# Agent attention with a squared-ReLU layer on one core: VectorE and ScalarE take over the element-wise work that GpSimd shared

## The chip, the core and the metric

The kernel runs on one core of a Trainium2 chip. The metric is the device time of one execution in microseconds (us). One execution was profiled; the times below name it apart from the other runs. Engine names: TensorE (PE in the rows, its weight loads PEld), VectorE (DVE), ScalarE (ACT), GpSimd (POOL), SyncE (SP, it issues the DMAs).

## The reference, cut to what matters

Four batches of 12480 tokens with 128 features, 49 agent tokens per batch, and a feed-forward layer of width 2048 behind the attention:

```python
a2k = sm(agents, k)                 # agents attend to the keys
agent_v = a2k @ v
q2a = sm(q, agents)                 # queries attend to the agents
x = (q2a @ agent_v).reshape(49920, 128)
h = np.maximum(x @ w_in, 0.0)
out = (h * h) @ w_out
```

All of it is float32. `sm` is a softmax of the scaled dot products.

## The kernel before, in words

The product `agent_v @ w_in` is made once per batch (the table `aw_hi`, with its low part `aw_ex`), so that a token's hidden values come straight from its 49 attention weights. Tokens go in blocks of 960, and each block in two halves of 480 columns; 52 blocks, 104 halves. The hidden width of 2048 is cut into 16 pieces of 128, two pieces make a slot, so a half has 8 slots and the kernel 832. Slots are grouped into sessions of 3, 3 and 2 (`SIZES`), three sessions per half.

One session of m slots does this:

- `first` (L351): 2m matmuls of the weights with `aw_hi` and 2m small ones with `aw_ex` (19 rows) into m PSUM tiles `h` of two banks. There are three such tiles, all of PSUM but the banks of `o` and `psa`.
- `squares` (L378): the rectifier of each slot into the tile `r`, then one square over the whole session on ScalarE. In a session of three, VectorE rectifies the first slot and ScalarE the other two.
- `halved` (L390): the squares are split in two parts that TensorE can take at full speed. `g_hi` is a rounding copy (VectorE). `g_lo` is the difference `r - g_hi`: the first m pieces of 480 columns on GpSimd (L394), one instruction each, and the other m pieces in one instruction on VectorE.
- `second` (L411): per piece of 128, two matmuls with `g_hi` (tables `wo_lo`, `wo_hi`) and, after all of those, one with `g_lo`, 6m in all, accumulated over the half in the one PSUM tile `o`. After the last session of a half `copied_out` (L401) copies `o` to `ob` on VectorE and sends it out; the next half's first `second` needs `o` back.

The order is written out by hand. `queued` chains each such instruction to the one before it on its engine. In step s of the main loop TensorE gets `first(s)` and then `second(s-2)` (`LAG = 2`); ScalarE gets rectifiers and squares of s; VectorE gets, in this order, the copy to `ob` if one is due and `halved(s-1)`.

Beside this runs the attention, as Python generators that are moved a step at a time: `queries` (scores of the block after next with the agents, softmax, splitting, transposes by TensorE, the copy `w`, then five DMAs per half that lay `w` out for the small matmuls) and `background` (scores, maxima, weighted values and tables of the next batch). They share the one PSUM bank `psa`. In the steady part `alone` is False, and then an instruction issued through `pe`, `act`, `dve`, `pool`, `sync` is not chained: the scheduler places it in its engine's queue where it expects its inputs to be ready. `tiled` matmuls are always chained. In `first`, a due step of `queries` or `background` is moved after the hidden matmuls, if the last transposes are more than a slot back or the session has three slots (`turns`).

```python
        for n in range(m):
            nc.gpsimd.tensor_sub(rest[:, n, :], r[:, n, :], near[:, n, :])
        n = slice(m, 2 * m)
        queued(nc.vector.tensor_sub, nc.vector, rest[:, n, :], r[:, n, :], near[:, n, :])
```

Of the kernel before, what the change touches and what calls it, by code (L numbers as in the profile page):

```python
# [18 lines left out]
TP = 120  # L19
# [2 lines left out]
KB = P * NT  # L22
G = BLK // 2
SIZES = (3, 3, 2)
WIDEST = max(SIZES)
RB = 3
HB = 2
# [14 lines left out]
def agent_attention_relu2(ctx: ExitStack, tc: tile.TileContext, qT, kT, v, agT, w_in, w_out, outT):  # L42
# [24 lines left out]
    alone = [True]  # L67

    class Ordered:
        def __init__(self, eng):  # L70
            self.eng = eng

        def __getattr__(self, name):
            issue = getattr(self.eng, name)
            if not alone[0]:
                return issue
            return lambda *args, **kw: queued(issue, self.eng, *args, **kw)

    pe, act, dve, pool, sync = (Ordered(e) for e in (nc.tensor, nc.scalar, nc.vector, nc.gpsimd, nc.sync))

    const = ctx.enter_context(tc.tile_pool(name="const", bufs=1))
    kv = ctx.enter_context(tc.tile_pool(name="kv", bufs=2))
# [100 lines left out]
    def scores(b, i, kt):  # L183
        st = state.setdefault(b, {"s": []})
        _, rows, nt = blocks[i]
        yield 3
        sv = bank()[:rows, : nt * NA].rearrange("p (t a) -> p t a", a=NA)
        for t in range(nt):
            tiled(sv[:, t, :], kt[:, t * rows : (t + 1) * rows], ag[:, b, :])
        s = sp.tile([P, 512], F32, name="s")[:, : NT * NA].rearrange("p (t a) -> p t a", a=NA)  # L190
        st["s"].append(s)
        if i == 0:
            st["mx"] = small.tile([P, NT, NA], F32, name="mx")
        s, mx = (x[:rows, :nt, :] for x in (s, st["mx"]))
        act.copy(s, sv)
        if i == 0:
            dve.tensor_copy(mx, s)
        else:
            dve.tensor_max(mx, mx, s)
# [48 lines left out]
    def values(b, i, vt):  # L248
        st = state[b]
        _, rows, nt = blocks[i]  # L250
        es = st["mx"][:rows, :nt, :]
        e = small.tile([P, NT, NA], F32, name="d", bufs=2)[:rows, :nt, :] if i else es
        less_maximum(b, i, e, pool)
        yield
        act.activation(e, e, AF.Exp, scale=scale)
        yield 3 if i else FIRST
        pv = bank()
        for t in range(nt):
            tiled(pv[:C, :NA], vt[:rows, t, :], e[:, t, :], start=(t == 0), stop=(t == nt - 1))
        if i == 0:  # L260
            st["av"] = small.tile([C, NA], F32, name="av")
            dve.tensor_copy(st["av"], pv[:C, :NA])
        else:
            dve.tensor_add(st["av"], st["av"], pv[:C, :NA])
            pool.tensor_add(es, es, e)  # L265

    def tables(b):
        st = state[b]
        rl, av = st["rl"], st["avT"]
        hi = st["hi"] = aw.tile([P, FF], F32R, name="aw_hi")  # L270
        ex = st["lo"] = aw.tile([P, NCH // NQ, P], F32R, name="aw_ex")
        for n in range(FF // 512):
            yield
            cs = slice(n * 512, (n + 1) * 512)
            pw = bank()
            pe.matmul(pw[:K2, :], av, win[:, cs], start=True, stop=True)
            yield
            act.activation(hi[:K2, cs], pw[:K2, :], AF.Copy, scale=rl)
            lo = aw.tile([P, 512], F32R, name="aw_lo", bufs=3)[:NA, :]
            dve.scalar_tensor_tensor(  # L280
                out=lo, in0=pw[:NA, :], scalar=rl[:NA, :], in1=hi[:NA, cs].bitcast(F32),
                op0=ALU.mult, op1=ALU.subtract,
            )
            yield
            sync.dma_start(hi[K2:, cs].bitcast(F32), lo[:SP, :].bitcast(F32))
            for t in range(NQ):
                sync.dma_start(ex[t * 32 : t * 32 + NL, n, :].bitcast(F32), lo[SP:, t * P : (t + 1) * P].bitcast(F32))


    weights = {}  # L290
    slot, turns = [0], [-2]

    def queries(g):
        b = g // NB
        qt = qp.tile([C, BLK], F32, name="qt", bufs=1)
        sync.dma_start(qt, qT[:, g * BLK : (g + 1) * BLK])
        yield 3
        ps = ps_a.tile([P, 512], F32, name="psa")
        sv = ps[:TP, : NT * NA].rearrange("p (t a) -> p t a", a=NA)
        for t in range(NT):  # L300
            tiled(sv[:, t, :], qt[:, t * TP : (t + 1) * TP], ag[:, b, :])
        if alone[0]:
            yield
        m = qp.tile([TP, NT, 1], F32, name="m", bufs=1)
        dve.reduce_max(m, sv, axis=AX.X)
        e = qp.tile([TP, NT, NA], F32, name="e", bufs=1)
        dve.tensor_sub(e, sv, m.broadcast_to([TP, NT, NA]))  # L307
        yield
        if not alone[0]:
            yield  # L310
        act.activation(e, e, AF.Exp, scale=scale)  # L311
        yield
        z = qp.tile([TP, NT, 1], F32, name="z", bufs=1)
        dve.reduce_sum(z, e, axis=AX.X)
        dve.tensor_scalar_add(z, z, 1e-9)
        dve.reciprocal(z, z)
        pool.tensor_mul(e, e, z.broadcast_to([TP, NT, NA]))  # L317
        yield
        pp = qp.tile([TP, NT, K2], F32R, name="pp", bufs=1)
        yield from halves(pp, e, NA, pool)  # L320
        weights[g] = []
        for j in range(2):
            yield
            pt = ps_a.tile([P, 512], F32, name="psa")
            turns[0] = slot[0]
            for t in range(NT // 2):
                pe.matmul(  # L327
                    pt[:K2, t * TP : (t + 1) * TP], pp[:, j * (NT // 2) + t, :], identr, start=True, stop=True
                )
            w = qp.tile([P, G], F32R, name=f"w{j}", bufs=2)  # L330
            x = qp.tile([P, G], F32R, name=f"x{j}", bufs=2)
            act.copy(w[:K2, :], pt[:K2, :G])  # L332
            weights[g].append((w, x))
            yield
            sync.dma_start(w[K2:, :].bitcast(F32), w[:SP, :].bitcast(F32))
            for t in range(NQ):
                sync.dma_start(x[t * 32 : t * 32 + NL, :].bitcast(F32), w[SP:NA, :].bitcast(F32))
# [9 lines left out]
    def first(k, m):  # L347
# [11 lines left out]
        with tc.high_priority():  # L359
            for n, out in outs:  # L360
                t = n % NQ
                rows = slice(t * 32, t * 32 + NL)
                queued(nc.tensor.matmul, nc.tensor, out, state[b]["lo"][rows, n // NQ, :], x[rows, :], start=False, stop=True)
        if turns[0] < k - 1 or m == WIDEST:
            for name in ("ahead", "todo"):
                if type(stands.get(name)) is int and k >= stands[name] and done[name] < goal[name]:
                    move(name, k)
                    break
        return hs

    def squares(hs, apart):

        m = len(hs)
        r = ffn.tile([P, WIDEST, 2, G], F32, name="r", bufs=RB)
        for x, h in enumerate(hs):
            if x == 0 and m == WIDEST:
                queued(nc.vector.tensor_scalar_max, nc.vector, r[:, x, :, :], h[:, :, :G], 0.0)
            else:  # L378
                queued(nc.scalar.activation, nc.scalar, r[:, x, :, :], h[:, :, :G], AF.Relu)
        for x in pieces(m, apart):  # L380
            queued(nc.scalar.activation, nc.scalar, r[:, x, :, :], r[:, x, :, :], AF.Square)
        return r

    def pieces(m, apart):
        return [slice(x, x + 1) for x in range(m)] if apart else [slice(0, m)]

    def halved(k, m, r, apart):
        hi = ffn.tile([P, WIDEST, 2, G], F32R, name="g_hi", bufs=HB)
        lo = ffn.tile([P, WIDEST, 2, G], F32R, name="g_lo", bufs=LB)
        for x in pieces(m, apart):  # L390
            queued(nc.vector.tensor_copy, nc.vector, hi[:, x, :, :], r[:, x, :, :])
        r, near, rest = (x.rearrange("p s n t -> p (s n) t") for x in (r, hi.bitcast(F32), lo))
        for n in range(m):
            nc.gpsimd.tensor_sub(rest[:, n, :], r[:, n, :], near[:, n, :])  # L394
        n = slice(m, 2 * m)
        queued(nc.vector.tensor_sub, nc.vector, rest[:, n, :], r[:, n, :], near[:, n, :])
        for x in range(m):
            parts[k + x] = hi[:, x, :, :], lo[:, x, :, :]

# [317 lines left out]
    following = [None]  # L717
    sessions, at = [], 0
    while at < total:
        for m in SIZES:  # L720
            sessions.append((at, m))
            at += m
    made, split = {}, {}
    for s in range(len(sessions) + LAG):
# [2 lines left out]
            behind = [chain[eng] for eng in (nc.tensor, nc.sync, nc.scalar, nc.vector, nc.gpsimd)]  # L727
        if m:
            between(k)
            hs = first(k, m)  # L730
        copied_out()
        if m:
            made[s] = squares(hs, s < LAG)
            if s < LAG:
                alone[0] = True
                if s:
# [4 lines left out]
            halved(*sessions[s - 1], made.pop(s - 1), s <= LAG)  # L741
        if s >= LAG:
            second(*sessions[s - LAG])
        for x in range(1, m):
            between(k + x)
    copied_out()
# [35 lines left out]
```

## Time and profile before

| what | value |
|---|---|
| median of 3 runs | 2259.98 us (2257.22 to 2265.25) |
| the profiled execution | 2256.87 us |
| its span | 2255.0 us |
| mean granted TensorE clock | 0.955 of full speed |
| busy: TensorE, VectorE, ScalarE, GpSimd | 89%, 72%, 64%, 76% |

The span runs from the first to the last instruction on the core; 1.87 us of the execution lie around it. Busy shares say how long an engine had an instruction in it, not how well the instruction ran: matmuls are pipelined and overlap, so their spacing tells more than their duration. In a timeline row, the square brackets give the idle time of the engine before the instruction and what ended it; "x6" merges six instructions of one kind.

### The profile page before, as it was taken

The numbers are of one execution on the slowest core, as the hardware profiler recorded it, in microseconds if no ns is written. First come the engines' busy times: TensorE is split into PE (matmuls) and PEld (weight loads), VectorE is DVE, ScalarE is ACT, GpSimd is POOL, SyncE is SP. The second block draws the span as 40 slices with busy tenths as digits, with TensorE's granted clock in tenths as the row PEclk, the third lists the DMA queues.
The fourth block names the chain that finished last, engine by engine and source line by source line (L and its number), as shares of the span: only waits on it lengthen the run. The fifth ranks groups of instructions, "written<-read, shape, count | busy, mean of one in ns | idle before, by whom it ended". The sixth has DMA issues, their size and how long they took to land.

```text
span 2255.0 us, 41091 instructions
## 1 busy us (share of the span) xinstructions
PE 2004.8 (89%) x17181; PEld 1534.7 (68%) x17181; DVE 1626.9 (72%) x1400; ACT 1453.7 (64%) x1309; POOL 1716.7 (76%) x1033
## 2 busy tenths in 40 slices
PE   8888888899998898899989899889998989998898
PEld 5577666666676676676767676667666767666676
DVE  7677767677767677667768677667777777776776
ACT  5566666666765666666766666566676666766664
POOL 3567778877877778887777777888777887887787
PEclk9899999999999999999999999889999999999999
DMA  9122212111112222121112121121111110111100
GB/s 337 57 74 68 65 57 76 55 58 45 35 56 68 59 63 76 54 66 60 33 35 67 57 74 48 54 73 57 34 41 39 33 41 28 38 38 36 39 22 20
DMA packets 54829, 131.55 MB, mean 58 GB/s; under 512 B 6508, under 2 KB 34828, under 8 KB 54644
## 3 DMA queue, kind: packets, MB, share of 16 engines
q1 hardware_dynamic: 54644, 128.93, 17.8%
q8 instruction: 135, 2.21, 0.4%
q14 instruction: 50, 0.41, 0.1%
HBM read 80.97 MB, written 25.56 MB: 47 GB/s over the span
## 4 chain that ended last, share of the span: by engine, by line
PE 38%; POOL 34%; DVE 10%; issue 9%; ACT 9%; DMA 0%; ACTq 0%; SPq 0%; POOLq 0%; DVEq 0%
POOL g_lo L394 29%; PE o L63 23%; PE h L63 12%; ACT r L63 7%; DVE g_hi L63 5%; POOL e L317 3%; DVE r L63 3%; PE psa L63 2%; ACT w L332 1%; POOL d L231 1%; DMA ahead<-in_kT 0%; DVE t L63 0%; DVE mx L63 0%; POOL mx L265 0%; POOL pp L225 0%
## 5 line engine op out<-in xcount | busy, mean ns | idle before, releaser
L394 POOL TENSOR_TENSOR g_lo<-r,g_hi 128x480 fp32r<-128x480 f32 x832 | 1475.8, 1802 | 458.1 <-DVE g_hi L63 393.2
L63 ACT ACTIVATE r<-h 128x960 f32<-128x960 f32 x624 | 571.3, 969 | 306.2 <-PE h L63 291.8
L63 ACT ACTIVATE r<-r 128x2880 f32<-128x2880 f32 (+2 forms) x316 | 733.6, 2323 | 11.1 <-DVE r L63 3.1
L63 PE MATMUL o<-g_hi,wo_lo 128*128 128x480 f32 x1664 | 693.1, 416 | 49.2 <-DVE ob L63 49.2
L63 PE MATMUL o<-g_hi,wo_hi 128*128 128x480 f32 x1664 | 656.6, 395 | 0.0
L63 DVE TENSOR_TENSOR g_lo<-r,g_hi 128x1440 fp32r<-128x1440 f32 (+1 forms) x312 | 594.4, 1905 | 6.7
L63 DVE TENSOR_SCALAR r<-h 128x960 f32<-128x960 f32 x208 | 240.7, 1157 | 466.1 <-PE h L63 432.0
L63 DVE CAST g_hi<-r 128x2880 fp32r<-128x2880 f32 (+2 forms) x316 | 513.5, 1626 | 20.0 <-ACT r L63 17.9
L63 PE MATMUL o<-g_lo,wo_hi 128*128 128x480 f32 x1664 | 433.9, 388 | 44.8 <-POOL g_lo L394 44.4
L63 PE MATMUL h<-w,aw_hi 128*128 128x480 f32 x1664 | 442.1, 392 | 28.0 <-ACT r L63 20.3
L63 PEld LDWEIGHTS o<-g_hi,wo_lo 128*128 128x128 f32 x1664 | 329.2, 198 | 158.0 <-DVE ob L63 63.1
L63 PEld LDWEIGHTS o<-g_lo,wo_hi 128*128 128x128 f32 x1664 | 318.3, 193 | 111.7 <-POOL g_lo L394 63.3
L63 PEld LDWEIGHTS h<-w,aw_hi 128*128 128x128 f32 x1664 | 311.5, 192 | 89.4 <-ACT r L63 29.4
L63 PEld LDWEIGHTS o<-g_hi,wo_hi 128*128 128x128 f32 x1664 | 330.4, 199 | 44.1 <-issue 0.7
L63 PE MATMUL h<-x,aw_ex 19*128 19x480 f32 x1664 | 199.4, 458 | 0.0
L223 ACT CAST pp<-e 120x392 fp32r<-120x392 f32 x51 | 26.8, 525 | 249.1 <-POOL e L317 249.1
L63 PEld LDWEIGHTS h<-x,aw_ex 19*128 19x128 f32 x1664 | 82.4, 184 | 106.2 <-issue 104.0
L63 DVE COPY ob<-o 128x480 f32<-128x480 f32 x104 | 67.4, 648 | 45.7 <-PE o L63 45.7
L327 PEld LDWEIGHTS psa<-identr,pp 120*98 120x98 f32 x408 | 50.2, 176 | 62.3 <-ACT w L332 36.7
L327 PE MATMUL psa<-identr,pp 120*98 120x120 f32 x408 | 55.6, 262 | 39.9 <-ACT w L332 26.7
L225 POOL TENSOR_TENSOR pp<-e,pp 120x392 fp32r<-120x392 f32 x51 | 62.4, 1223 | 24.8 <-ACT pp L223 24.8
L311 ACT ACTIVATE e<-e 120x392 f32<-120x392 f32 x51 | 27.1, 531 | 82.5 <-DVE e L307 82.5
(143 smaller groups left out, 940.9 us busy)
## 6 DMA issues: line engine op xcount, KB each, us to landing
qt<-in_qT SPq DMA_DIRECT2D x52, 480.0 KB
out_T<-ob SPq DMA_DIRECT2D x104, 240.0 KB
kt<-in_kT SPq DMA_DIRECT2D x36, 512.0 KB
vt<-in_v SPq DMA_DIRECT2D x36, 512.0 KB
x<-w SPq DMA_DIRECT2D x416, 35.6 KB
ahead<-in_kT SPq DMA_DIRECT2D x12, 512.0 KB
ahead<-in_v SPq DMA_DIRECT2D x12, 512.0 KB
w<-w SPq DMA_DIRECT2D x104, 56.2 KB
```

The lines of the kernel that those rows point to most:

```text
L63: ins = issue(*args, **kw)
L223: act.copy(out[:, :, :w], x)
L225: eng.tensor_sub(out[:, :, n : n + w], x, out[:, :, :w].bitcast(F32))
L231: eng.tensor_sub(out, st["s"][i][:rows, :nt, :], mb)
L311: act.activation(e, e, AF.Exp, scale=scale)
L317: pool.tensor_mul(e, e, z.broadcast_to([TP, NT, NA]))
L327: pe.matmul(pt[:K2, t * TP : (t + 1) * TP], pp[:, j * (NT // 2) + t, :], identr, start=True, stop=True)
L332: act.copy(w[:K2, :], pt[:K2, :G])
L394: nc.gpsimd.tensor_sub(rest[:, n, :], r[:, n, :], near[:, n, :])
```

## The change

Seven edits. GpSimd keeps its work only while `alone` is True, that is, before the steady part; afterwards `spare()` is VectorE, and so four small subtractions, products and sums of the attention go there. `halved` makes the whole low part in one VectorE instruction per session. All rectifiers go to ScalarE, and they are issued inside `first`, ahead of the attention step that may follow there. The transposes of `queries` are chained, and their step waits (`"turn"`) until a `second` has been issued, directly behind which it is moved. Three ScalarE copies out of `psa` are chained (`fixed`). The condition with `turns` goes. The first half of all is cut into four sessions of two slots (`EARLY`).

```diff
+EARLY = (2, 2, 2, 2)
...
+    fixed = Ordered(nc.scalar, True)
+
+    def spare():
+        return pool if alone[0] else dve
...
-        act.copy(s, sv)
+        fixed.copy(s, sv)
...
-        less_maximum(b, i, e, pool)
+        less_maximum(b, i, e, spare())
...
-            pool.tensor_add(es, es, e)
+            spare().tensor_add(es, es, e)
...
-            act.activation(hi[:K2, cs], pw[:K2, :], AF.Copy, scale=rl)
+            fixed.activation(hi[:K2, cs], pw[:K2, :], AF.Copy, scale=rl)
...
-        pool.tensor_mul(e, e, z.broadcast_to([TP, NT, NA]))
+        spare().tensor_mul(e, e, z.broadcast_to([TP, NT, NA]))
         yield
         pp = qp.tile([TP, NT, K2], F32R, name="pp", bufs=1)
-        yield from halves(pp, e, NA, pool)
+        yield from halves(pp, e, NA, spare())
         weights[g] = []
         for j in range(2):
-            yield
+            yield "turn"
             pt = ps_a.tile([P, 512], F32, name="psa")
-            turns[0] = slot[0]
             for t in range(NT // 2):
-                pe.matmul(
-                    pt[:K2, t * TP : (t + 1) * TP], pp[:, j * (NT // 2) + t, :], identr, start=True, stop=True
+                queued(
+                    nc.tensor.matmul, nc.tensor, pt[:K2, t * TP : (t + 1) * TP], pp[:, j * (NT // 2) + t, :], identr, start=True, stop=True
                 )
...
-            act.copy(w[:K2, :], pt[:K2, :G])
+            fixed.copy(w[:K2, :], pt[:K2, :G])
...
-        if turns[0] < k - 1 or m == WIDEST:
-            for name in ("ahead", "todo"):
-                if type(stands.get(name)) is int and k >= stands[name] and done[name] < goal[name]:
-                    move(name, k)
-                    break
-        return hs
-
-    def squares(hs, apart):
-
-        m = len(hs)
         r = ffn.tile([P, WIDEST, 2, G], F32, name="r", bufs=RB)
         for x, h in enumerate(hs):
-            if x == 0 and m == WIDEST:
-                queued(nc.vector.tensor_scalar_max, nc.vector, r[:, x, :, :], h[:, :, :G], 0.0)
-            else:
-                queued(nc.scalar.activation, nc.scalar, r[:, x, :, :], h[:, :, :G], AF.Relu)
+            queued(nc.scalar.activation, nc.scalar, r[:, x, :, :], h[:, :, :G], AF.Relu)
+        for name in ("ahead", "todo"):
+            if type(stands.get(name)) is int and k >= stands[name] and done[name] < goal[name]:
+                move(name, k)
+                break
+        return r
+
+    def squares(m, r, apart):
         for x in pieces(m, apart):
             queued(nc.scalar.activation, nc.scalar, r[:, x, :, :], r[:, x, :, :], AF.Square)
-        return r
...
-        r, near, rest = (x.rearrange("p s n t -> p (s n) t") for x in (r, hi.bitcast(F32), lo))
-        for n in range(m):
-            nc.gpsimd.tensor_sub(rest[:, n, :], r[:, n, :], near[:, n, :])
-        n = slice(m, 2 * m)
-        queued(nc.vector.tensor_sub, nc.vector, rest[:, n, :], r[:, n, :], near[:, n, :])
+        for x in pieces(m, apart):
+            queued(nc.vector.tensor_sub, nc.vector, lo[:, x, :, :], r[:, x, :, :], hi[:, x, :, :].bitcast(F32))
...
-        for m in SIZES:
+        for m in SIZES if at else EARLY:
...
         if s >= LAG:
             second(*sessions[s - LAG])
+            if stands.get("ahead") == "turn":
+                move("ahead", slot[0])
```

## Rows read from the trace of the kernel before

**Rows 1.** The page: busy time, share of the span and instructions of each engine.
```profile
PE 2004.8 (89%) x17181; PEld 1534.7 (68%) x17181; DVE 1626.9 (72%) x1400; ACT 1453.7 (64%) x1309; POOL 1716.7 (76%) x1033
```

**Rows 2.** The page: the chain that ended last, by engine and by line.
```profile
PE 38%; POOL 34%; DVE 10%; issue 9%; ACT 9%; DMA 0%; ACTq 0%; SPq 0%; POOLq 0%; DVEq 0%
```

**Rows 3.** Tile ob: count, duration min/median/max in ns, first and last start; whole span, last quarter.
```profile
L63 DVE COPY ob<-o x104: 639/647/659, 101.7 to 2251.5; 128x480 f32<-128x480 f32 x104
...
L63 DVE COPY ob<-o x24: 641/650/658, 1800.3 to 2251.5; 128x480 f32<-128x480 f32 x24
```

**Rows 4.** Waits, all engines: who waited for whom, us in total, times, longest us.
```profile
POOL g_lo L394 <- DVE g_hi L63: 393.2, 144, 15.6
...
ACT pp L223 <- POOL e L317: 249.1, 51, 8.0
...
PE o L63 <- DVE ob L63: 49.2, 44, 1.7
...
PE o L63 <- POOL g_lo L394: 44.4, 30, 2.1
```

**Rows 5.** Timeline of TensorE, 1833 to 1856 us: start, duration, engine, line, operation.
```profile
1836.62 0.48 PE L327 MATMUL psa<-identr,pp 120*98 120x120 f32 x4
1836.94 1.09 PE L63 MATMUL h<-w,aw_hi 128*128 128x480 f32 x4
...
1843.52 1.12 PE L63 MATMUL o<-g_lo,wo_hi 128*128 128x480 f32 x4 [0.95 <-POOL g_lo L394]
1844.48 1.47 PE L63 MATMUL h<-w,aw_hi 128*128 128x480 f32 x6
...
1850.55 1.46 PE L63 MATMUL h<-w,aw_hi 128*128 128x480 f32 x6
...
1852.57 0.90 PE L63 MATMUL psa<-ag,qt 128*32 128x49 f32 x64
```

**Rows 6.** Timeline of TensorE, 605 to 632 us.
```profile
620.60 1.50 PE L63 MATMUL o<-g_lo,wo_hi 128*128 128x480 f32 x4 [2.08 <-POOL g_lo L394]
621.90 2.60 PE L63 MATMUL h<-w,aw_hi 128*128 128x480 f32 x6
```

**Rows 7.** Groups by form, the attention's matmuls: count, busy us, mean ns, idle before.
```profile
L63 PE MATMUL psa<-ag,qt 128*32 128x49 f32 x2496 | 47.2, 210 | 0.0
...
L63 PE MATMUL psa<-ag,kt 128*32 128x49 f32 x2340 | 36.5, 218 | 38.2 <-ACT w L332 21.6 <-issue 14.3 <-DVE e L307 2.3
L63 PE MATMUL psa<-d,vt 128*32 128x49 f32 x2112 | 35.7, 228 | 23.9 <-ACT w L332 13.1 <-issue 10.7
```

**Rows 8.** Groups by form, the element-wise work of the sessions.
```profile
L394 POOL TENSOR_TENSOR g_lo<-r,g_hi 128x480 fp32r<-128x480 f32 x832 | 1475.8, 1802 | 458.1 <-DVE g_hi L63 393.2 <-ACT r L63 21.3 <-DVE av L264 10.4
...
L63 ACT ACTIVATE r<-h 128x960 f32<-128x960 f32 x624 | 571.3, 969 | 306.2 <-PE h L63 291.8 <-POOL g_lo L394 14.4
L63 ACT ACTIVATE r<-r 128x2880 f32<-128x2880 f32 x206 | 539.3, 2618 | 8.3 <-DVE r L63 3.1
...
L63 DVE TENSOR_SCALAR r<-h 128x960 f32<-128x960 f32 x208 | 240.7, 1157 | 466.1 <-PE h L63 432.0 <-POOL g_lo L394 30.8 <-POOL mx L231 3.2
```

**Rows 9.** Timeline of VectorE, 1828 to 1862 us.
```profile
1835.28 1.66 DVE L63 CAST g_hi<-r 128x2880 fp32r<-128x2880 f32 x1 [0.24 <-ACT r L63]
1836.98 1.66 DVE L63 TENSOR_TENSOR g_lo<-r,g_hi 128x1440 fp32r<-128x1440 f32 x1
...
1840.17 2.23 DVE L63 CAST g_hi<-r 128x2880 fp32r<-128x2880 f32 x1 [0.96 <-ACT r L63]
1842.44 2.54 DVE L63 TENSOR_TENSOR g_lo<-r,g_hi 128x1440 fp32r<-128x1440 f32 x1
...
1849.47 1.16 DVE L63 TENSOR_TENSOR g_lo<-r,g_hi 128x960 fp32r<-128x960 f32 x1
...
1855.17 0.56 DVE L305 TENSOR_REDUCE m<-psa 120x8 f32<-120x392 f32 x1
...
1858.11 0.55 DVE L307 TENSOR_TENSOR e<-psa,m 120x392 f32<-120x392 f32 x1
```

**Rows 10.** Tile z: count, duration min/median/max in ns.
```profile
L315 DVE TENSOR_SCALAR z<-z x51: 165/1184/1196, 92.4 to 2182.7; 120x8 f32<-120x8 f32 x51
```

More of the change, by code (lines that the diff above doesn't have):

```diff
@@ L69, in agent_attention_relu2, with __init__ @@
     class Ordered:
-        def __init__(self, eng):
-            self.eng = eng
+        def __init__(self, eng, always=False):
+            self.eng, self.always = eng, always
         def __getattr__(self, name):
             issue = getattr(self.eng, name)
-            if not alone[0]:
+            if not (alone[0] or self.always):
                 return issue
@@ L290, in agent_attention_relu2 @@
     weights = {}
-    slot, turns = [0], [-2]
+    slot = [0]
     def queries(g):
@@ L729, in agent_attention_relu2 @@
             between(k)
-            hs = first(k, m)
+            made[s] = first(k, m)
         copied_out()
         if m:
-            made[s] = squares(hs, s < LAG)
+            squares(m, made[s], s < LAG)
             if s < LAG:
```

## The prediction, made before the changed kernel was run

> **What bounds the kernel now.** I read the busy shares first. TensorE stands at 89% and GpSimd at 76%, and no engine is full [rows 1]. The chain that ended last is split between TensorE (38%) and GpSimd (34%) [rows 2], so the end is set by an exchange between the two. The copies to `ob` then give the beat: 104 of them, the first at 101.7 us and the last at 2251.5, so 103 halves at 2149.8 / 103 = 20.87 us; in the last quarter, with no further batch to prepare, 23 halves in 451.2 us, 19.62 each [rows 3]. The waits say who holds whom: GpSimd waits 393 us for `g_hi`, ScalarE's rounding copy `pp` waits 249 us in its queue for GpSimd's product `e`, and TensorE waits for `g_lo` and for `ob` [rows 4].
>
> What would TensorE need if nothing held it? The 89% cannot tell. In the timeline a session of three slots takes from one `h` group to the next 1850.55 - 1844.48 = 6.07 us with no wait inside [rows 5]. A session of two has two thirds of the instructions, 4.05. A half is 2 x 6.07 + 4.05 = 16.2 us. The attention adds groups of 64 small matmuls at 0.90 us [rows 5]: 52 for queries (2496 / 48), 37 for keys (2340 / 64), 33 for values (2112 / 64) [rows 7], 110 us; and 102 groups of transposes at 1836.94 - 1836.62 = 0.32, 33 us. That is 1.4 per half. So TensorE needs **17.6 us** of the 20.87, and 3.3 per half are waits and slow clock. The Trainium skill warns of this very reading (Trainium Kernel Development and Optimization, Performance Expectations: matmul busy time is a bad measure of closeness, because matmuls are pipelined). Taken as work, 2004.8 us of busy time would allow no less than 19.3 us per half, and the sum below would end near 2100.
>
> The slow clock hangs on the waits: behind a wait of 2.08 us six `h` matmuls took 2.60 us, behind one of 0.95 they took 1.47 [rows 5, 6], the first at the 1.2 GHz level, the second at 2.4.
>
> **The change part by part.**
>
> *GpSimd's low parts.* 832 instructions of 1802 ns go [rows 8]; the second of two sessions of three waits for six in a row. What replaces them is one VectorE instruction per session, 2880 elements wide in a session of three, which no row shows. The nearest are 1.16 us for 960 and 1.66 for 1440 [rows 9], so 0.5 per 480, which gives 1.66 + 1.5 = **3.16 us**. The same form also took 2.54 [rows 9], when GpSimd was inside an instruction at its start; doubled that is 5.0, the upper end. Below 3.1 there is no reason to go. I take 3.16, since GpSimd will be idle; that the delay is GpSimd's, the 8-element instruction on `z` says, which takes 165 ns at best and 1184 in the median [rows 10].
>
> *Rectifiers.* VectorE loses 208 x 1157 ns, ScalarE gains 208 x about 0.92 (571.3 / 624, back to back) [rows 8]. VectorE is spared 2.3 us per half that stood ahead of a rounding copy; a session's three rectifiers now run one behind the other, 2.75 us where ScalarE's two took 1.83. They hide beside TensorE's `second` of 18 matmuls, about 3.9 us; if ScalarE comes late, `h` comes free late and the next `first` waits.
>
> *Four attention steps to VectorE.* 51 products, 51 differences, 36 differences and 33 sums, 171 at 0.55 (as `e` [rows 9]), 0.9 us per half. VectorE then has per half 2 x (1.66 + 3.16), two thirds of 4.82 for the small session, 0.65 for `ob`, 0.9, and some 1.5 of attention that it had: 15.9 us. ScalarE has (1453.7 + 191) / 104 = 15.8. Both lie under 17.6, so neither bounds by its sum; both are covers that get thin.
>
> *Transposes and `turn`.* Four matmuls, the copy `w` and then five DMAs on SyncE's queue move behind a `second`. Counting the steps, one per slot, the two turns fall in the second half of a block, at its first and second session, and the last DMAs are issued four slots before the weights are read, half a period or some 9 us. I cost them at nothing for the time; without that cover the first matmul of a block would wait. The chained ScalarE copies wait behind the squares ahead of them, and the next user of `psa` waits with them; it comes a `first` later, at least 1.3 us. Of the 249 us that `pp` waited for GpSimd [rows 4] I count nothing twice: they end in the waits already counted.
>
> *First half in two-slot sessions.* One more hand-over, smaller pieces, once; between -3 and +5 us, taken as 0: the first `ob` stays at 101.7.
>
> **What is late next.** The copy to `ob`. Once per half the accumulator must be copied before the next half's `second`. VectorE has the copy behind the whole `halved` of a three-slot session. From the moment that session's `h` is done: 2.75 rectifiers, 2.62 square [rows 8], 1.66 rounding copy, 3.16 low part, 0.65 `ob`, and some 0.25 for hand-overs: 11.1 us. TensorE meanwhile does a `second` and a `first` of three and of two: 6.07 + 4.05 = 10.1. It waits 1.0. In every other half the scores of a query lie in this stretch (TensorE +0.9), but `m` and `e` also come onto VectorE ahead of the copy (0.56 + 0.55 [rows 9]): wait 1.2. In the others two transposes lie in it (0.64): wait 0.4. On average 0.8 us, short enough that by the pair above the clock stays up.
>
> **The sum.** 17.6 + 0.8 = 18.4 us per half. 101.7 + 103 x 18.4 + 3.5 (behind the last `ob`) = 2000 us of span; with 1.9 around it 2002. The profiled execution lies 3.1 under the median of the runs, so the forecast for the median is **2005 us**, 11% less.
>
> **The rivals.**
>
> (1) *The background falls on the chain* (25%). The chain of 11.1 us runs through ScalarE and VectorE, and unchained attention steps are put into both queues by expectation. For it: `pp` stood waiting on ScalarE for 4.9 us on average (249.1 / 51 [rows 4]), and both engines now run at 86% of the new period. If half of the 1.5 us of ScalarE's and 2.4 of VectorE's attention work per half lands in it, that adds 1.9, of which TensorE's own background hides some: 1.2. Then 19.6 per half, 2005 + 103 x 1.2 = 2129. Against it: much of VectorE's time behind `ob` is free. The Trainium skill leans to this side (ScalarE: Activation LUTs, Rules for kernel authors: for relu use VectorE, not ScalarE). This trace has it the other way for this shape, 969 ns on ScalarE against 1157 on VectorE [rows 8]; only the load of ScalarE speaks for the rule.
>
> (2) *Everything is hidden* (14%). TensorE's background covers the wait for `ob` wholly: 17.6 per half, 1923.
>
> (3) *VectorE stays at its slow price* (9%), the other side. If not GpSimd but something that remains slows VectorE, the low part costs 5.0 and the rounding copy 2.23 [rows 9]. Per half: 2 x 7.23 + 4.8 + 0.65 + 2.4 = 22.3 us, VectorE is the bound, and the time is 101.7 + 103 x 22.3 + 8.5 = 2407. It decides from where VectorE's sum passes 20.87, a low part of about 5 us with the copy at 1.66, and 4.5 with it at 2.23. Against it are the short instances beside the long ones [rows 9, 10].
>
> (4) *The waits only change their names* (4%). The scheduler puts unchained steps where GpSimd's delay was; 20.8 per half, no difference.
>
> **How the numbers follow.** The forecast's own case, 18.0 to 18.9 per half or 1964 to 2057, has 48%. The range takes in the better part of (1), whose price I know least, and the upper part of (2): 1935 to 2150, that is 17.7 to 19.8 per half, some 8 in 10. Runs of this kernel differ by some 0.3%, which is what a measurement can tell from no change. Faster by more: 48 + 25 + 14 = 87%. The same: 4%. Slower: 9%.
>
> **What would show it.** GpSimd under 40 us. The low part of 2880 at 3.1 to 3.2 us on VectorE and the 8-element step on `z` near 165 ns throughout; if the first is near 5, (3) holds. VectorE and ScalarE each busy some 1640 to 1660 us. Halves by the distance of the `ob` copies at 18.4, under 17.7 in the last quarter. TensorE's waits for `g_lo` gone and those for `ob` the longest kind, about one per half and mostly under 1.3 us; waits of `h` for ScalarE's `r` instead would be (1). Granted clock at 0.98 or more. Wrong altogether I would be if TensorE spends more than 6.1 us on a session of three with no wait in it.

## The result, and the profile after

The median went from 2259.63 us to 2103.29 us (2101.62 to 2105.91, 4 runs): a ratio of 0.9306 with an interval of 0.9286 to 0.9326. The kernel is 6.9% faster; 11% was forecast, and 2103 lies inside the range.

The page of the changed kernel, busy time and the chain by engine, answering to [rows 1, 2]:

```profile
span 2099.6 us, 39766 instructions
PE 1959.2 (93%) x17181; PEld 1508.9 (72%) x17181; DVE 1640.4 (78%) x1371; ACT 1637.7 (78%) x1516; POOL 20.6 (1%) x24
...
PE 55%; ACT 18%; DVE 17%; issue 9%; DMA 1%; SPq 0%; POOL 0%; ACTq 0%; DVEq 0%; POOLq 0%
```

GpSimd has left the chain, TensorE has more than half of it, and VectorE and ScalarE carry most of the rest, in equal parts.

The groups by form (busy us, mean ns, then idle time before), answering to [rows 8], and the small step on `z` (min/median/max), answering to [rows 10]:

```profile
L64 ACT ACTIVATE r<-h 128x960 f32<-128x960 f32 x832 | 752.0, 973 | 290.5 <-PE h L64 287.5 <-POOL s L64 0.7
...
L64 DVE TENSOR_TENSOR g_lo<-r,g_hi 128x2880 fp32r<-128x2880 f32 x206 | 649.7, 3154 | 9.7 <-PE psa L64 0.9
...
L64 DVE CAST g_hi<-r 128x2880 fp32r<-128x2880 f32 x206 | 341.4, 1657 | 282.9 <-ACT r L64 274.0 <-PE o L64 7.9
```

```profile
L321 DVE TENSOR_SCALAR z<-z x51: 159/163/173, 83.1 to 2033.4; 120x8 f32<-120x8 f32 x51
```

The low part costs what was said, 3.15 us, and VectorE's instructions are short throughout. VectorE now waits for ScalarE's squares (274 us ahead of the rounding copy), so it has room on the average; that it has none in one place, the experiments show.

The copies to `ob`, answering to [rows 3], and two stretches with the granted clock in the column behind POOL (then the DMAs' busy share and GB/s):

```profile
L64 DVE COPY ob<-o x104: 644/649/659, 90.9 to 2096.0; 128x480 f32<-128x480 f32 x104
```

```profile
90.90:1606.10 1515.20, 1434.03 (x13710) 1113.56 (x13710) 1215.49 (x1015) 1210.64 (x1105) 0.00 (x0) 0.98 0.19 62
1606.10:2096.00 489.90, 449.31 (x2772) 345.90 (x2771) 356.79 (x250) 367.39 (x312) 0.00 (x0) 0.94 0.10 33
```

103 halves took 2005.1 us, 19.47 each against the 18.4 forecast. The last quarter, 25 halves in 489.9 us, takes 19.6 each, as much as it took before (19.62 [rows 3]), and it has the lower clock, although it has the least to do. So that is the place to look first. Its halves alternate; the copies to `ob` on VectorE:

```profile
1784.94 0.65 DVE L64 COPY ob<-o 128x480 f32<-128x480 f32 x1
...
1807.59 0.66 DVE L64 COPY ob<-o 128x480 f32<-128x480 f32 x1 [5.42 <-PE o L64]
...
1825.84 0.65 DVE L64 COPY ob<-o 128x480 f32<-128x480 f32 x1
```

One half of 22.65 us, one of 18.25; VectorE stands 5.42 us ready before the long one's copy, so the copy is not what is late. The same stretch in time order, all engines:

```profile
1787.54 0.55 DVE L320 TENSOR_REDUCE z<-e 120x8 f32<-120x392 f32 x1
...
1791.08 0.16 DVE L321 TENSOR_SCALAR z<-z 120x8 f32<-120x8 f32 x1
...
1792.22 0.19 DVE L322 RECIPROCAL z<-z 120x8 f32<-120x8 f32 x1
...
1794.48 0.56 DVE L323 TENSOR_TENSOR e<-e,z 120x392 f32<-120x392 f32 x1
1796.84 0.50 ACT L229 CAST pp<-e 120x392 fp32r<-120x392 f32 x1
1796.97 1.66 DVE L64 CAST g_hi<-r 128x2880 fp32r<-128x2880 f32 x1 [1.93 <-ACT r L64]
1798.55 0.56 DVE L231 TENSOR_TENSOR pp<-e,pp 120x392 fp32r<-120x392 f32 x1
...
1799.16 0.56 PE L64 MATMUL psa<-identr,pp 120*98 120x120 f32 x4 [3.31 <-DVE pp L231]
1799.56 1.80 PE L64 MATMUL h<-w,aw_hi 128*128 128x480 f32 x6
...
1805.75 1.80 PE L64 MATMUL o<-g_lo,wo_hi 128*128 128x480 f32 x4
```

The first chained transposes wait 3.31 us for VectorE's difference `pp`, and all of TensorE's chain waits behind them. `pp` is late in every queue that it passes. The four steps of the softmax's end, from the sum `z` to the product `e`, are spread over 7 us of VectorE's queue; ScalarE then starts its rounding copy `pp` 1.8 us behind the product's end; and the difference `pp` stands behind a rounding copy that itself waited for squares. Behind the wait the clock falls: four `o` matmuls take 1.80 us where they took 1.12 [rows 5], and the granted clock of these 7.9 us is 0.60, near the lower of its two levels (1.2 of 2.4 GHz is 0.50):

```profile
1799.10:1807.00 7.90, 7.84 (x28) 5.74 (x29) 3.07 (x2) 5.43 (x5) 0.00 (x0) 0.60 0.07 19
```

TensorE's longest waits over the whole kernel, answering to [rows 4]:

```profile
PE psa L64 <- DVE pp L231: 62.5, 32, 3.3
PE psa L64 <- DVE aw_lo L286: 21.7, 6, 6.6
...
PE o L64 <- DVE ob L64: 6.9, 24, 0.6
```

The waits for `g_lo` are gone, and those for `ob` nearly. In their place stand waits for `pp` (11 of the 32, and 36.3 of the 62.5 us, lie in the last quarter) and for the bank `psa` while the tables are copied out of it.

### The profile page after: what moved, and what is told of

Read it like the earlier page. It is cut to its first block, busy times and chain, and to the rows that moved or that the text cites. A ratio compares the mean times of both kernels' runs of the same rounds, so it can differ in the third digit from the quotient of the medians.

```text
span 2099.6 us, 39766 instructions
## 1 busy us (share of the span) xinstructions
PE 1959.2 (93%) x17181; PEld 1508.9 (72%) x17181; DVE 1640.4 (78%) x1371; ACT 1637.7 (78%) x1516; POOL 20.6 (1%) x24
## 4 chain that ended last, share of the span: by engine, by line
PE 55%; ACT 18%; DVE 17%; issue 9%; DMA 1%; SPq 0%; POOL 0%; ACTq 0%; DVEq 0%; POOLq 0%
PE o L64 32%; PE h L64 18%; ACT r L64 17%; DVE g_hi L64 7%; DVE g_lo L64 5%; PE psa L64 4%; DVE ob L64 1%; DVE pp L231 1%; DVE m L311 1%; DVE z L320 0%; DVE t L64 0%; DVE e L323 0%; DMA ahead<-in_kT 0%; DVE mx L64 0%; DMA x<-w 0%
## 5 line engine op out<-in xcount | busy, mean ns | idle before, releaser
L64 ACT ACTIVATE r<-h 128x960 f32<-128x960 f32 x832 | 752.0, 973 | 290.5 <-PE h L64 287.5
L64 DVE TENSOR_TENSOR g_lo<-r,g_hi 128x2880 fp32r<-128x2880 f32 (+2 forms) x315 | 880.4, 2796 | 15.0 <-PE psa L64 0.9
L64 DVE CAST g_hi<-r 128x2880 fp32r<-128x2880 f32 (+2 forms) x315 | 464.9, 1476 | 291.8 <-ACT r L64 282.7
L64 PE MATMUL o<-g_hi,wo_lo 128*128 128x480 f32 x1664 | 682.5, 410 | 7.1 <-DVE ob L64 6.9
L64 PE MATMUL o<-g_hi,wo_hi 128*128 128x480 f32 x1664 | 647.6, 389 | 0.0
L64 PE MATMUL h<-w,aw_hi 128*128 128x480 f32 x1664 | 426.2, 387 | 0.4 <-DVE aw_hi L64 0.4
L64 PE MATMUL psa<-identr,pp 120*98 120x120 f32 x416 | 54.9, 256 | 72.8 <-DVE pp L231 62.5
L64 ACT CAST w<-psa 98x480 fp32r<-98x480 f32 x104 | 57.2, 550 | 50.0 <-PE psa L64 50.0
L64 PE MATMUL psa<-ag,qt 128*32 128x49 f32 (+1 forms) x3328 | 48.4, 213 | 26.2 <-DVE aw_lo L286 21.7
L64 PEld LDWEIGHTS psa<-ag,qt 128*32 128x32 f32 (+1 forms) x3328 | 41.1, 111 | 43.2 <-DVE aw_lo L286 24.2
L231 DVE TENSOR_TENSOR pp<-e,pp 120x392 fp32r<-120x392 f32 x51 | 28.8, 564 | 21.0 <-ACT pp L229 21.0
## 6 DMA issues: line engine op xcount, KB each, us to landing
x<-w SPq DMA_DIRECT2D x416, 35.6 KB
```

Source lines behind the costliest of these rows:

```text
L64: ins = issue(*args, **kw)
L231: eng.tensor_sub(out[:, :, n : n + w], x, out[:, :, :w].bitcast(F32))
```

## The experiments

Each kernel was timed beside the kernel before on the same chip. The ratio is to that kernel; the changed kernel itself stands at 0.9306.

| run | edit | median us | ratio (interval) |
|---|---|---|---|
| the change | | 2103.29 | 0.9306 (0.9286 to 0.9326) |
| e1 | change, turn one session later | 2276.3 | 1.0057 (1.0038 to 1.0075) |
| e2 | change, tables' copy unchained | 2099.01 | 0.9267 (0.9251 to 0.9282) |
| e3 | e1 and e2 | 2247.26 | 0.9921 (0.989 to 0.9951) |
| e4 | change, transposes free | 2249.16 | 0.9933 (0.9915 to 0.995) |
| e5 | before, low parts on VectorE | 2232.01 | 0.9871 (0.9844 to 0.9898) |
| e6 | before, transposes chained at a turn | 2231.44 | 0.9884 (0.985 to 0.9918) |
| e7 | change, end of softmax chained | 2010.13 | 0.8896 (0.8873 to 0.8918) |
| e8 | change, rectifier back on VectorE | 2256.7 | 0.998 (0.9965 to 0.9996) |
| e9 | change, 1.2 us of idle work on VectorE | 2294.09 | 1.0143 (1.0121 to 1.0165) |
| e10 | change, attention steps on GpSimd | 2092.0 | 0.9249 (0.923 to 0.9268) |
| e12 | e7 and e2 | 1980.04 | 0.8758 (0.8743 to 0.8773) |

**The turn one session later (e1).**

```diff
         weights[g] = []
+        if not alone[0]:
+            yield
         for j in range(2):
             yield "turn"
```

> The changed kernel with one more slot step between the difference pp and the first turn, so that the chained transposes come one session later; nothing else. Theory A (chained transposes make TensorE wait for pp): the 11 waits of some 3.3 us in the last quarter and the 30 of some 1.25 us before go, and with them the 1.2 GHz stretches behind them; the last quarter's halves all take 17.3 to 18.3 us instead of 18.2 and 22.6 in turn; 2103 falls to 2030 to 2050. Rival B (TensorE would wait at that place anyway, for the copy to ob or for free h tiles): the wait for pp goes, another of the same length stands in its place, 2095 to 2105.

2276.3 us: 173 us slower than the change, a clear miss of both theories. The wait for `pp` did go, but the DMAs behind the transposes lost their cover. TensorE's longest wait, and one place of it in TensorE's timeline, where the small matmuls of a new block's first session come, the first of them at 1939.12:

```profile
PE h L64 <- DMA x<-w: 100.1, 114, 1.8
```

```profile
1940.09 0.48 PE L64 MATMUL h<-x,aw_ex 19*128 19x480 f32 x1 [0.49 <-DMA x<-w]
1941.68 0.50 PE L64 MATMUL h<-x,aw_ex 19*128 19x480 f32 x1 [1.11 <-DMA x<-w]
1943.13 0.77 PE L64 MATMUL h<-x,aw_ex 19*128 19x480 f32 x3 [0.94 <-DMA x<-w]
```

The four DMAs of the first turn were issued from 1934.89 us on, one at a time; of the small matmuls, which otherwise run together, the second, third and fourth each waited for one. So the turn has room neither forward (`pp`) nor backward (the DMAs): a session later costs more than the wait it saves.

**The tables' copy unchained (e2), and both (e3).**

```diff
-            fixed.activation(hi[:K2, cs], pw[:K2, :], AF.Copy, scale=rl)
+            act.activation(hi[:K2, cs], pw[:K2, :], AF.Copy, scale=rl)
```

> The changed kernel with the ScalarE copy of the tables (aw_hi) unchained again, as before the change; nothing else. Theory A (chained, it stands behind the squares of a session and holds the bank psa, and the scores chained on TensorE wait 6.6 us for it): the half of 29 us at each of the three batch ends falls to about 20, 2103 falls by 25 to 30, to about 2075. Rival B (the tables hold the bank that long in any case): within 5 us of 2103.

2099.01 us, rival B by the time. Yet the wait did shrink, from 21.7 us to 4.1; the one for `pp` grew from 62.5 to 71.4, and the mean granted clock went from 0.969 to 0.966. So most of what was gained went into that wait and the clock.

> Both edits of the two runs before together. Theory A: the gains add, 2000 to 2025, which is the time that was predicted for the change without these two waits. Rival B: 2090 or more. If the sum of the two single gains comes out clearly larger than the gain here, they are parts of one wait.

2247.26 us: e1's loss again, and here the copy is worth 29 us (2276.3 - 2247.26). What a removed wait is worth depends on which other wait stands next to it.

**The transposes free (e4).**

```diff
-            yield "turn"
+            yield
...
-                queued(
-                    nc.tensor.matmul, nc.tensor, pt[:K2, t * TP : (t + 1) * TP], pp[:, j * (NT // 2) + t, :], identr, start=True, stop=True
+                pe.matmul(
+                    pt[:K2, t * TP : (t + 1) * TP], pp[:, j * (NT // 2) + t, :], identr, start=True, stop=True
...
-            fixed.copy(w[:K2, :], pt[:K2, :G])
+            act.copy(w[:K2, :], pt[:K2, :G])
```

> The changed kernel with the transposes and the copy w unchained and without the turn, as before the change; the rest stays changed. Theory A: no instruction of TensorE's chain stands behind pp any more, so the last quarter loses its halves of 22.6 us; but the scheduler may again put the transposes where psa is still held, with waits of 1 to 2 us as in the kernel before: 2040 to 2080. Rival B: 2095 to 2110. Rival C (the fixed place was itself a gain over the free one): over 2110.

2249.16 us, rival C: the fixed place is worth 146 us to the change. TensorE's waits without it:

```profile
PE psa L332 <- ACT w L337: 63.5, 27, 3.1
PE psa L64 <- ACT w L337: 50.7, 30, 3.2
PE h L64 <- DMA x<-w: 39.6, 47, 1.2
```

Placed by expectation, the transposes hold `psa` until ScalarE gets round to `w`, and the DMAs come late. The condition with `turns`, which held other steps back behind the transposes in the kernel before, is not in this kernel; no run shows how much of the 146 us is due to its absence.

**The low part alone (e5) and the turn alone (e6), on the kernel before.**

```diff
-        for n in range(m):
-            nc.gpsimd.tensor_sub(rest[:, n, :], r[:, n, :], near[:, n, :])
-        n = slice(m, 2 * m)
-        queued(nc.vector.tensor_sub, nc.vector, rest[:, n, :], r[:, n, :], near[:, n, :])
+        for x in pieces(m, apart):
+            n = slice(2 * x.start, 2 * x.stop)
+            queued(nc.vector.tensor_sub, nc.vector, rest[:, n, :], r[:, n, :], near[:, n, :])
```

> The kernel before, with one edit: the whole low part on VectorE (GpSimd keeps the four attention steps, VectorE keeps its rectifiers, the transposes stay free). Theory L (the low part is what bound the kernel, as the prediction had it): TensorE's waits for g_lo go and the time falls to 2100 to 2180. Theory T (the fixed place of the transposes is the main gain, and without it the time goes into waits of the transposes, of psa and of the DMAs x): 2230 to 2270. VectorE is busy some 1850 us, its low part of 2880 at 3.2 to 4 us.

2232.01 us, theory T's time. The waits for `g_lo` went, as theory L had it, but TensorE waited for the copy to `ob` and for `psa` instead:

```profile
PE o L63 <- DVE ob L63: 88.8, 49, 2.3
PE psa L63 <- ACT w L332: 44.1, 29, 1.9
```

```diff
-            yield
+            yield "turn"
...
-                pe.matmul(
+                queued(
+                    nc.tensor.matmul, nc.tensor,
...
-            act.copy(w[:K2, :], pt[:K2, :G])
+            fixed.copy(w[:K2, :], pt[:K2, :G])
...
             second(*sessions[s - LAG])
+            if stands.get("ahead") == "turn":
+                move("ahead", slot[0])
```

> The kernel before, with one edit: transposes and copy w chained, moved at a turn behind a second; low parts and rectifiers stay as they were before. Theory T: 2100 to 2160. Theory L: 2230 to 2260, GpSimd's low parts still set the beat. Theory I (each needs the other: with GpSimd's slow product and difference, pp comes later still, and a chained transpose waits for it longer than 3.3 us): over 2260.

2231.44 us, theory L's time, with the wait of theory I in it (TensorE for `pp` 57.8 us) beside `ob` (60.9) and `g_lo` (52.9). Neither part brings more than 1.3% alone. Taken out of the change, the turn costs 146 us (e4) and a quarter of the rectifiers 153 (e8, next), together more than the 156 us that the change gains: the parts need each other. That each removes a wait which hides the next fits this; the rectifiers alone were not moved in the kernel before.

**The rectifier back on VectorE (e8).**

```diff
-            queued(nc.scalar.activation, nc.scalar, r[:, x, :, :], h[:, :, :G], AF.Relu)
+            if x == 0 and m == WIDEST:
+                queued(nc.vector.tensor_scalar_max, nc.vector, r[:, x, :, :], h[:, :, :G], 0.0)
+            else:
+                queued(nc.scalar.activation, nc.scalar, r[:, x, :, :], h[:, :, :G], AF.Relu)
```

> The changed kernel with the first rectifier of a session of three back on VectorE; nothing else. VectorE is busy 1880 us, ScalarE 1450. Theory C (VectorE's queue carries the chain rectifier, square, rounding copy, low part, copy to ob; 1.16 us ahead of each rounding copy lengthens it by about 1 us per half, and VectorE runs at some 90%): 2170 to 2230. Rival D (ScalarE's three rectifiers in a row cost as much as VectorE's one): within 15 us of 2103.

2256.7 us: beyond theory C's range, the whole gain gone with one of the three rectifiers of a session of three. ScalarE, VectorE and TensorE around one copy to `ob`:

```profile
1798.75 2.62 ACT L64 ACTIVATE r<-r 128x2880 f32<-128x2880 f32 x1
```

```profile
1802.84 1.16 DVE L64 TENSOR_SCALAR r<-h 128x960 f32<-128x960 f32 x1 [1.60 <-PE h L64]
1803.91 1.65 DVE L64 CAST g_hi<-r 128x2880 fp32r<-128x2880 f32 x1
...
1809.50 0.65 DVE L64 COPY ob<-o 128x480 f32<-128x480 f32 x1
```

```profile
1810.20 0.77 PE L64 MATMUL o<-g_hi,wo_lo 128*128 128x480 f32 x1 [2.27 <-DVE ob L64]
1810.76 0.60 PE L64 MATMUL o<-g_hi,wo_hi 128*128 128x480 f32 x1
1811.16 0.60 PE L64 MATMUL o<-g_hi,wo_lo 128*128 128x480 f32 x1
```

The squares of the session are done at 1801.37. Their rounding copy starts at 1803.91, because the next session's rectifier stands ahead of it in VectorE's queue, and that one waits 1.60 us for `h`. The low part and `ob` come as much later, TensorE waits 2.27 us, and goes on with 0.40 us from matmul to matmul, the 1.2 GHz level. Over the kernel TensorE waits 112.4 us for `ob`, 68 times.

**The same work without the wait (e9).**

```diff
+        if m == WIDEST:
+            two = [t.rearrange("p c d -> p (c d)")[:, :G].bitcast(F32) for t in (wo_hi, wo_lo)]
+            for _ in range(2):
+                queued(nc.vector.tensor_sub, nc.vector, even[:, :G], two[0], two[1])
         for x, h in enumerate(hs):
```

> The changed kernel with two VectorE differences of 480 elements of constant tables (into a tile that nobody reads any more, some 1.2 us together) at the place where the rectifier stood in a session of three, ahead of the rounding copy of the session before. It gives VectorE the load of the rectifier without its wait for TensorE's h; ScalarE keeps all rectifiers. Theory W (what the rectifier cost on VectorE was its wait for h, ahead of a rounding copy whose squares were long done): within 40 us of 2103. Theory L (the 1.2 us of work lengthen the chain that ends in the copy to ob): 2200 to 2260, as with the rectifier itself.

2294.09 us, slower than with the rectifier. Theory W falls by the time. Theory L falls by the mechanism (and 2294 lies above its range), for `ob` is hardly waited for:

```profile
PE psa L64 <- DVE pp L231: 168.6, 47, 6.1
...
PE o L64 <- DVE ob L64: 14.3, 28, 1.5
```

So the two costs of an instruction at this place part: a wait for `h` makes `ob` late (e8), work alone makes `pp` late (e9), and the turn is chained behind `pp`. In e8 itself TensorE's wait for `pp` was only 21.6 us, less than the change's 62.5, so there the first cost seems to cover the second. Where VectorE's load bites without the rectifier should then be the end of the softmax, which the next run tries.

**The end of the softmax chained (e7).** If that is so, `pp` is to be made earlier, not the turn later.

```diff
+        if not alone[0]:
+            yield
         z = qp.tile([TP, NT, 1], F32, name="z", bufs=1)
-        dve.reduce_sum(z, e, axis=AX.X)
-        dve.tensor_scalar_add(z, z, 1e-9)
-        dve.reciprocal(z, z)
-        spare().tensor_mul(e, e, z.broadcast_to([TP, NT, NA]))
-        yield
+        steady.reduce_sum(z, e, axis=AX.X)
+        steady.tensor_scalar_add(z, z, 1e-9)
+        steady.reciprocal(z, z)
+        (pool if alone[0] else steady).tensor_mul(e, e, z.broadcast_to([TP, NT, NA]))
+        if alone[0]:
+            yield
```

with `steady = Ordered(nc.vector, True)`: the four steps follow one another, where before a rounding copy or a low part had stood between every two of them. They also begin a slot later, and ScalarE's copy `pp` follows in the same step.

> The changed kernel with the end of the queries' softmax (sum z, its two small steps, the product) chained on VectorE one slot later, so that no wide instruction stands between its steps, and pp ahead of the next rounding copy of a session of three. Theory A (TensorE's wait for pp is a true loss): waits for pp in the last quarter fall from 3.3 us to under 1, its halves from 22.6 to at most 19, and the time to 2040 to 2065. Rival B (the wait stands where the copy to ob would have stood): 2090 to 2105.

2010.13 us, below theory A's range and 4.4% under the change (0.8896 / 0.9306 = 0.956). The sum `z` and the product `e` now start about 1 us apart, where it was 6.9; then TensorE's wait for `pp`, and the last quarter with its clock:

```profile
1775.09 0.55 DVE L64 TENSOR_REDUCE z<-e 120x8 f32<-120x392 f32 x1
...
1776.12 0.57 DVE L64 TENSOR_TENSOR e<-e,z 120x392 f32<-120x392 f32 x1
```

```profile
PE psa L64 <- DVE pp L232: 4.9, 15, 0.4
```

```profile
1580.00:2009.90 429.90, 418.26 (x2754) 324.71 (x2752) 360.32 (x250) 363.02 (x311) 0.00 (x0) 1.00 0.11 38
```

The clock of the last quarter is full (1.00 after 0.94). Over the kernel the wait for `pp` is 57.6 us shorter (62.5 - 4.9), and the mean granted clock went from 0.969 to 0.988; what both make of the time stands in the sum below.

**Once more, and with the tables (e11, e12).** The run e11 has the kernel of e7 unchanged, whatever its label says; the first half in sessions of two was not undone in any run.

> The kernel with the chained end of the softmax once more, unchanged, to tell how far one look lies from the run before: 2008 to 2013.

2009.34 us, a single execution, 0.8 us from e7's median.

> The chained end of the softmax and the unchained copy of the tables together. If the long half at each batch end (28 to 29 us) is a wait of its own, it falls to about 20 and the time from 2010 to 1980 to 1990. If it only moves to the next half, as it did without the chained softmax: 2003 to 2010.

1980.04 us, as expected if the wait is its own. The same edit that brought 4 us in e2 brings 30 once `pp` no longer waits. This version is 12% faster than the kernel before and 5.9% faster than the change (0.8758 / 0.9306 = 0.941).

**The attention steps on GpSimd (e10).**

```diff
-        return pool if alone[0] else dve
+        return pool
```

> The changed kernel with the four attention steps back on GpSimd; low parts stay on VectorE, rectifiers on ScalarE, transposes chained. VectorE is busy some 90 us less by the work. Theory S (these steps were moved because GpSimd makes pp late, and its two-input instructions hold up VectorE): pp comes 1 to 2 us later, the chained transposes wait longer, 2110 to 2160. Rival (VectorE's load is what counts): 2060 to 2095.

2092.0 us, the rival's side, at the edge of its range: 0.6% faster than the change, the intervals just apart. The chained transposes did not wait longer: TensorE's wait for `pp` is 42.0 us, where the change has 62.5. GpSimd idle in the steady part is no gain in itself: on those four steps the load taken from VectorE weighs a little more than GpSimd's longer instructions.

## Why the prediction was right in part

**One sum for four of them.** All these kernels give TensorE the same 17181 matmuls. Take from each span the time that TensorE was not busy (span less busy time) and the slow clock ((1 - mean granted clock) x span). The lines for it, of the kernel with the chained end of the softmax (e7) and of the one with the tables too (e12), are span, TensorE's busy time and mean clock:

```profile
span 2009.9 us, 39793 instructions
PE 1920.0 (96%) x17181; PEld 1487.5 (74%) x17181; DVE 1652.2 (82%) x1371; ACT 1632.4 (81%) x1516; POOL 20.7 (1%) x24
core 0: 2009.9 us, clock 0.988
```

```profile
span 1978.4 us, 39792 instructions
PE 1910.8 (97%) x17181; PEld 1481.4 (75%) x17181; DVE 1650.5 (83%) x1371; ACT 1632.7 (83%) x1516; POOL 20.7 (1%) x24
core 0: 1978.4 us, clock 0.995
```

| kernel | span | not busy | slow clock | what is left |
|---|---|---|---|---|
| before | 2255.0 | 250 | 0.045 x 2255.0 = 101 | 1904 |
| the change | 2099.6 | 140 | 0.031 x 2099.6 = 65 | 1894 |
| e7 | 2009.9 | 90 | 0.012 x 2009.9 = 24 | 1896 |
| e12 | 1978.4 | 68 | 0.005 x 1978.4 = 10 | 1901 |

What is left agrees within 10 us, so waits and the clock that falls behind them account for the differences between the four. The sum is rougher for the others, from 1865 us (e9) to 1915 (e6); for one thing, time in which TensorE stands idle at the low clock is taken off twice.

The prediction's floor of 17.6 us per half holds within 0.2: in e12, whose granted clock is 0.995, the halves take (1974.8 - 92.1) / 103 = 18.3, and TensorE is busy 1833.8 us in that stretch, 17.8 per half. The conclusion that the prediction drew from the Trainium skill (Trainium Kernel Development and Optimization, Performance Expectations) came out: the busy time of the same matmuls was 2004.8 us before and is 1910.8 in e12, so it was not work that had to remain. The Trainium skill gives the pipelining of the matmuls as its reason; here the difference of 94 us is about that of the column "slow clock", 101 - 10. That the change's 2103 lies close to the 2100 worked out from the busy time is therefore no sign of a floor.

**The low part: right.** 3.16 us taken, 3.154 measured; the upper end, 5.0, and rival (3) fall with it. That the slow instances were GpSimd's doing is shown by `z`: 163 ns in the median after 1184 [rows 10]; in e5, where nothing but the low part left GpSimd, it is 165.

**The rectifiers: right in what they cost ScalarE, too small in what they gave.** 752.0 / 832 = 0.90 us each against 0.92. Counted for VectorE were 2.3 us per half of work; e8 shows that the wait for `h` in front of a rounding copy counted too, and that the whole gain can be lost by it. The rule of the Trainium skill that was set against it (ScalarE: Activation LUTs, Rules for kernel authors) would have kept the rectifier on VectorE. The measurement decides: for this float32 tile 973 ns stand against 1157 [rows 8], and the kernel that follows the rule with one rectifier of three is as slow as the kernel before (e8).

**The copy to `ob`: wrong.** It was to be late by 0.8 us per half, 82 us. TensorE waited 6.9 us for it. That is not because the wait for `pp` hid it: without that wait TensorE waits 9.3 us for `ob` in e7 and 9.1 in e12. A half of the change with scores, around the copy at 1825.84 shown above, has the term that was too large:

```profile
1815.15 2.69 ACT L64 ACTIVATE r<-h 128x960 f32<-128x960 f32 x3 [2.22 <-PE h L64]
...
1825.36 0.56 DVE L311 TENSOR_REDUCE m<-psa 120x8 f32<-120x392 f32 x1
...
1826.40 0.55 DVE L313 TENSOR_TENSOR e<-psa,m 120x392 f32<-120x392 f32 x1
...
1826.54 0.49 PE L64 MATMUL o<-g_hi,wo_lo 128*128 128x480 f32 x1 [0.24 <-DVE ob L64]
```

From the rectifiers to the end of the copy it took 11.3 us, where 11.1 + 1.1 = 12.2 had been added up: the step `e` came behind the copy, not ahead of it, and the hand-overs cost next to nothing. TensorE had 11.1 us of work in it (11.0 was said) and waited 0.24 instead of 1.2. For the halves with a turn this stays open. As a mechanism the wait is real where VectorE also has the rectifier, in e8 (112.4 us) and e5 (88.8).

**Transposes and turn: the step that failed.** "I cost them at nothing." They wait 62.5 us for `pp`, chained, so that all of TensorE's queue waits with them, and behind the wait of 3.3 us shown above the granted clock was 0.60. e7 takes that wait away: 93 us. The sign "under 17.7 in the last quarter", which failed with 19.6, holds there: the last 31 copies to `ob` lie between 1490.0 and 2006.3 us, 17.2 per half. Of the other side the step had the mechanism (without its cover the first matmul of a block waits for the DMAs), and e1 shows it at 100.1 us of waits; the cover was said to be some 9 us deep, and in e1 the last matmul was let go 8.2 us after the first DMA was issued (1943.13 - 1934.89), so there was no session of 4 to 6 us to give away. What was not seen at all is that the fixed place is a gain of 146 us over the free one (e4).

**The chained copies: wrong for the tables.** "It comes a `first` later, at least 1.3 us." The scores behind the tables waited 21.7 us for `psa` in six places, 6.6 at the longest; removed beside e7 it gives 30 us (e12). The chained copy of the keys' scores was not freed in any run.

**The clock: wrong.** 0.98 or more was to be seen, and 0.969 was: the waits left were few and long, not many and short.

**The first half: better than its bounds.** The first `ob` came at 90.9 us, 10.8 earlier; 0 was taken, between -3 and +5. In all runs with `EARLY` it came at 91 to 94 us, in e5 and e6, without it, at 102.3 and 101.4. So the two go together over many kernels, but no run made this edit by itself, and the cause is not shown.

**The numbers.** 103 x (19.47 - 18.4) = 110, less 10.8 at the start, makes the 98 us between 2005 and 2103, but for 1 us. The forecast's own case (1964 to 2057) missed; the range held because it took in rival (1), and partly by luck, for the terms that were wrong went against each other: the 82 us at `ob` and the start were too dear, the transposes and the tables cost nothing in the sum. Rival (1) comes nearest by time (2129), by another place: the background did fall on the way, but on TensorE's own chain by way of `pp`, not on the way to `ob`. Something of rival (4) is in it too: waits did change their names.

## What to carry to other kernels

A chained instruction on the engine that bounds the kernel is priced by the latest of its inputs, followed back to the queue in which that input waits; "it is moved" is no price. Where several waits stand close together, one removed alone can show little (here 1.2 and 1.3% in e6 and e5, 4 us in e2 where the same edit brought 30 in e12), so a part that brings nothing alone is not yet worthless. And of a small instruction in an in-order queue ask first what it waits for and what stands behind it; its duration comes second.

## What the runs showed of the hardware that was not expected

An 8-element VectorE instruction took 1184 ns in the median while GpSimd made its share of the low part, 165 when only that was taken from GpSimd (e5), and 163 with GpSimd idle. A TensorE wait of 2.27 us was followed by matmuls 0.40 us apart (e8), the 1.2 GHz level; one of 0.95 us was not [rows 5]. And of four DMAs of 35.6 KB inside the on-chip memory, issued some 0.6 us apart, the last three let their matmuls go at 1940.09, 1941.68 and 1943.13 us, 1.6 and 1.5 us apart (e1): the landing, not the issue, set the pace.
